# Attention with soft expert routing on one core: slot inputs from 128-token products, x turned in 32-row groups on VectorE

## The chip, the core and the metric

The kernel runs on one core of a Trainium2 chip. Its engines work side by side, each through its own queue in order: TensorE (PE; its weight loads are listed apart as PEld), VectorE (DVE), ScalarE (ACT), GpSimd (POOL) and SyncE (SP), which issues the DMAs. Engines wait for each other by semaphores. The metric is the device time of one execution in microseconds.

## The reference

Eight batches of attention with sigmoid weights give x, one row per token. A soft mixture of experts follows: every one of 32 slots is a softmax-weighted mean over all tokens, eight experts with four slots each transform the slots, and every token is a softmax-weighted mean of the slot outputs.

```python
scores = q @ k.T / sqrt(64) - log(448)              # B=8, H=12, S=448, head 64
attn = 1 / (1 + exp(-scores));  x = attn @ v        # x: 3584 tokens x 768
logits = x @ phi                                    # 3584 x 32 slots
d = exp(logits - logits.max(0)); d /= d.sum(0) + 1e-9
slot_input = d.T @ x                                # 32 x 768, over all tokens
h = relu(slot_input[e] @ w1[e]); slot_out[e] = h @ w2[e]   # 8 experts, 4 slots each
c = exp(logits - logits.max(1)); c /= c.sum(1) + 1e-9
out = c @ slot_out                                  # 3584 x 768, all float32
```

## The kernel before

**Attention.** Heads go in pairs: `p` counts 48 pairs, six to a batch, and x of a pair is a tile of 128 rows (two heads of 64) by 448 tokens, so channels lie on the partitions. Keys go in chunks of 128; the 64 keys left over of two neighbouring pairs share a unit (`c == NFK`, tiles `vl`). `seq` lists the units, seven per two pairs and 21 per batch. The loop of line 365 makes one pass per unit: `score(u)` (four products in 64x64 tiles of TensorE into a PSUM tile `sc`, then one sigmoid on ACT), and, two units later (`LAG`), `weigh(u)` (four products into `av0` for an even pair or `av1` for an odd one). `sc` has two buffers, `av0` and `av1` one each. After a pair's last full chunk `evac_a` copies the first half of its sum to `xr`; when the other half is there, `evac_b` adds it. For an even pair the second comes one pass later, behind the left-over keys; for an odd pair at once.

**Slots.** After a batch, `logits_job` multiplies phi with x into four groups of 32 rows: row 32j + s holds slot s over a share of the tokens given by `COLS`. Each of the 128 rows keeps its own running maximum in `mz` (`softmax_a`), and `softmax_b` forms exp on ACT from two sigmoids, `softmax_c` ends it on DVE. `turn` transposes x of a pair in place by 32x32 blocks on DVE, six instructions of 128x448 per batch. `spread` writes the weights to DRAM and reads them back four times, once for each group of 32 partitions, since `slot_mm` multiplies in 32x32 tiles: 56 products of 32x192 per batch, into two PSUM tiles. `slot_job` adds them to `acc` after scaling. For the last batch `last_job` does all this without the bounce, brings the four maxima of a slot together, and forms `sT`, the slot inputs.

**Order.** PE, DVE, ACT and SP run in the order of the program text. The tables `early`, `middle` and `late` (lines 352 to 363) say in which pass, counted from a batch's end, each job is written.

**Experts and output.** 56 of 128 weight tiles are loaded during attention; eleven more take the place of attention's buffers, and the others follow as tiles come free. `w1_part` (line 430), `w2_step` and `out_tile` run over them.

Of the kernel before, what the change touches and what calls it, by code (L numbers as in the profile page):

```python
# [18 lines left out]
P = 128  # L19
NFK = 3  # L20
LAG = 2
W_STEPS = 140
# [15 lines left out]
SL0 = 256  # L38
COLS = (0, 128, 256, 352, 448)
# [7 lines left out]
def soft_moe_attention(ctx: ExitStack, tc: tile.TileContext, qk, v, vl, phi, w1, w2, cst, out):  # L47
# [12 lines left out]
    mz = cpool.tile([P, 2], F32, name="mz")  # L60
    rz = cpool.tile([P, 1], F32, name="rz")
    lt_all = cpool.tile([P, B, P], F32, name="lt_all")
    sT = cpool.tile([P, NKC, NSLOT], F32, name="sT")
    acc = small.tile([P, DM], F32, name="acc")
    phi_t = small.tile([P, 256], F32, name="phit")
    phi_sb = phi_t[:, 0:NKC * NSLOT].rearrange("p (k s) -> p k s", k=NKC)
    nc.vector.memset(acc[:, 0:S], 0.0)
# [28 lines left out]
    with ExitStack() as actx:  # L96
# [4 lines left out]
        bounce = actx.enter_context(tc.tile_pool(name="bounce", bufs=2, space=bass.MemoryType.DRAM))  # L101
# [3 lines left out]
        xr = xp.tile([P, 3, 3, S], F32, name="xr")  # L105
        lgs = xp.tile([P, P], F32, name="lgs")
        nc.vector.memset(lgs[64:128, 96:128], NEG)
        qkts, vts, vls, avs, atts, dts, drs = {}, {}, {}, {}, {}, {}, {}

        def x_of(p):  # L110
            b, hp = divmod(p, NPR)
            return xr[:, (2 * b + hp // 3) % 3, hp % 3, :]
# [56 lines left out]
        def evac_a(p):  # L169
            nc.vector.tensor_copy(x_of(p), avs[p][:, 1, 0:S])  # L170
# [5 lines left out]
        def evac_last(p):  # L176
            x, av = x_of(p), avs.pop(p)
            for t in (slice(0, COLS[2]), slice(COLS[2], S)):
                nc.scalar.copy(x[:, t], av[:, 1, t])
# [5 lines left out]
        def turn(p):  # L185
            nc.vector.transpose(x_of(p), x_of(p))  # L186

        def logits(lg, b, pairs, js=(3, 2, 1, 0)):
            for hp in pairs:
                for j in js:  # L190
                    nc.tensor.matmul(  # L191
                        lg[32 * j:32 * j + 32, 0:COLS[j + 1] - COLS[j]], phi_sb[:, hp, :],
                        x_of(b * NPR + hp)[:, COLS[j]:COLS[j + 1]],
                        start=(hp == 0), stop=(hp == NPR - 1))

        def logits_job(b):
            lg = ps_sc.tile([P, 2, 512], F32, name="sc")[:, 0, :]
            logits(lg, b, range(NPR))
            nc.vector.tensor_copy(lgs[0:64, :], lg[0:64, 0:P])
            nc.vector.tensor_copy(lgs[64:128, 0:96], lg[64:128, 0:96])  # L200
            softmax_a(b)

        def softmax_a(b):
            t1 = small.tile([P, 2, 132], F32, name="t1")
            zt, ls = t1[:, 0, :], lgs[:]
            if b == 0:
                nc.vector.tensor_reduce(out=mz[:, 0:1], in_=ls, axis=AX.X, op=ALU.max)
            else:
                m1 = small.tile([P, 2], F32, name="m1")
                nc.vector.tensor_reduce(out=m1[:, 0:1], in_=ls, axis=AX.X, op=ALU.max)  # L210
                nc.vector.tensor_copy(m1[:, 1:2], mz[:, 0:1])
                nc.vector.tensor_tensor(out=mz[:, 0:1], in0=m1[:, 0:1], in1=m1[:, 1:2], op=ALU.max)
                nc.vector.tensor_tensor(out=zt[:, P:P + 1], in0=m1[:, 1:2], in1=mz[:, 0:1], op=ALU.subtract)
            nc.vector.tensor_scalar(zt[:, 0:P], ls, mz[:, 0:1], None, op0=ALU.subtract)
            dts[b] = t1
# [7 lines left out]
        def softmax_c(b):  # L223
# [5 lines left out]
            if b == 0:  # L229
                nc.vector.tensor_reduce(out=mz[:, 1:2], in_=pe[:, 0:P], axis=AX.X, op=ALU.add)  # L230
            else:
# [3 lines left out]
                    out=mz[:, 1:2], in0=mz[:, 1:2], scalar=pe[:, P:P + 1], in1=zb[:], op0=ALU.mult, op1=ALU.add)  # L235
            nc.vector.transpose(lt_all[:, b, :], lgs[:])

        def spread(b):
            flat = bounce.tile([P, P], F32, name="zd")
            nc.sync.dma_start(flat[:], dts[b][:, 0, 0:P])  # L240
            drs[b] = xp.tile([P, 4, NBK * BLK], F32, name="dr")
            for a in range(4):
                nc.sync.dma_start(drs[b][32 * a:32 * a + 32, :, :], flat[:].rearrange("(j i) n -> i j n", j=4))

        def slot_mm(b, sl=None):
            if sl is None:
                sl = [ps_av.tile([P, 2, 512], F32, name="av1"), ps_sc.tile([P, 2, 512], F32, name="sc")]
            t = 2 * b % 3
            y = xr[:, t:t + 2] if t < 2 else xr[:, 2::-2]
            for c in range(NBK):  # L250
                for a in range(4):
                    for j in range(4 if c < 3 else 2):
                        k = COLS[j] // BLK + c
                        nc.tensor.matmul(  # L254
                            sl[a // 2][32 * j:32 * j + 32, a % 2, SL0:SL0 + NPR * BLK],
                            drs[b][32 * a:32 * a + 32, j, c * BLK:(c + 1) * BLK],
                            y[32 * a:32 * a + 32, :, :, k * BLK:(k + 1) * BLK],
                            start=(c == 0), stop=(c == (3 if j < 2 else 2)))
            return sl

        def acc_of(g):
            return acc[:, g * HALF:(g + 1) * HALF].rearrange("p (a n) -> p a n", a=2)

        def slot_job(b):
            sl = slot_mm(b)
            for g in range(2):
                part = sl[g][:, :, SL0:SL0 + NPR * BLK]
                if b == 0:
                    nc.vector.tensor_copy(acc_of(g), part)
                else:  # L270
                    nc.vector.scalar_tensor_tensor(
                        out=acc_of(g), in0=acc_of(g), scalar=dts[b][:, 1, P:P + 1], in1=part,
                        op0=ALU.mult, op1=ALU.add)

        def last_job(b, lgt, pw):
            lg = lgt[:, 0, 0:P]
            pa = lgt[:, 1, :]
            ps = pw[:, 0, 0:NKC * NSLOT]
            t1 = small.tile([P, 2, 132], F32, name="t1")
            pe, zt = t1[:, 0, 0:P], t1[:, 1, 0:P]  # L280
            m1 = small.tile([P, 2], F32, name="m1")
            cw = small.tile([P, 8 + 2 * NSLOT], F32, name="cw")
            sw = cw[:, 8:].rearrange("p (z s) -> p z s", z=2)
            nc.vector.tensor_reduce(out=m1[:, 0:1], in_=lg, axis=AX.X, op=ALU.max)
            nc.vector.tensor_scalar(cw[:, 0:1], m1[:, 0:1], mz[:, 0:1], -1.0, op0=ALU.max, op1=ALU.mult)
            nc.scalar.activation(pe, lg, AF.Exp, bias=cw[:, 0:1])
            nc.scalar.activation(cw[:, 1:2], mz[:, 0:1], AF.Exp, bias=cw[:, 0:1])
            nc.tensor.matmul(pa[0:1, 0:P], cw[:, 0:1], ident, start=True, stop=True)
            warm(pw, 1)
            turn(b * NPR + 5)  # L290
            nc.vector.transpose(zt, pe)
            tr = [ps_av.tile([P, 2, 512], F32, name="av1"), ps_sc.tile([P, 2, 512], F32, name="sc")]
            for j in range(4):
                r = slice(32 * j, 32 * j + 32)
                nc.tensor.matmul(tr[j // 2][:, j % 2, 0:P], csb[r, 128:256], zt[r, :], start=True, stop=True)
            mrow = small.tile([1, 1, NSLOT], F32, name="mrow")
            nc.vector.tensor_reduce(
                out=mrow[:], in_=pa[0:1, 0:P].rearrange("o (j s) -> o s j", j=4), axis=AX.X, op=ALU.min)
            drs[b] = xp.tile([P, 4, NBK * BLK], F32, name="dr")
            nc.scalar.copy(drs[b][:, 0:2, :], tr[0][:, :, 0:P])  # L300
            nc.vector.tensor_copy(drs[b][:, 2:4, :], tr[1][:, :, 0:P])
            for j in range(4):
                nc.tensor.matmul(pa[32 * j:32 * j + 32, P:P + 1], mrow[:, 0, :], csb[0:1, 0:1], start=True, stop=True)
            slot_mm(b, tr)
            nc.vector.tensor_tensor(out=cw[:, 2:3], in0=pa[:, P:P + 1], in1=cw[:, 0:1], op=ALU.subtract)
            nc.scalar.activation(cw[:, 3:4], cw[:, 2:3], AF.Exp)
            nc.vector.tensor_scalar(sw[:, 0], sel4, cw[:, 3:4], None, op0=ALU.mult)
            nc.vector.tensor_scalar(sw[:, 1], sw[:, 0], cw[:, 1:2], None, op0=ALU.mult)
            total = xr[:, 1, 0:2, :].rearrange("p a n -> p (a n)")[:, 0:DM]
            for g, copy in enumerate((nc.scalar.copy, nc.vector.tensor_copy)):  # L310
                copy(total[:, g * HALF:(g + 1) * HALF].rearrange("p (a n) -> p a n", a=2),
                     tr[g][:, :, SL0:SL0 + NPR * BLK])
            for a in range(4):
                nc.tensor.matmul(
                    ps[32 * a:32 * a + 32, :], sw[:, 1], acc[:, a * 192:a * 192 + 192], start=True, stop=False)
            for a in range(4):
                nc.tensor.matmul(  # L317
                    ps[32 * a:32 * a + 32, :], sw[:, 0], total[:, a * 192:a * 192 + 192], start=False, stop=True)
            nc.vector.transpose(sT[:].rearrange("p k s -> p (k s)"), ps)
# [3 lines left out]
                out=cw[:, 5:6], in0=mz[:, 1:2], scalar=cw[:, 1:2], in1=cw[:, 4:5], op0=ALU.mult, op1=ALU.add)  # L323
# [290 lines left out]
```

## Time and profile before

| | |
|---|---|
| median of 3 runs | 397.16 us (396.82 to 438.41) |
| the profiled execution | 398.36 us, span of its instructions 396.6 us, mean granted clock 0.968 |
| busy over the span | PE 371.8 us, ACT 204.1, DVE 159.1, POOL 2.3 |
| DMA queue 1 | 96.92 MB, 71.1% of the 16 engines' span |
| slot products (L254) | 896 records, 36.1 us of busy time |
| transposes of x (L186) | 48, 27.8 us on DVE |
| copies of x (L170) and adds (L174) on DVE | 47 each, 29.4 and 28.9 us |
| bounce of slot weights | 7 writes and 28 reads of 64 KB |

Each group of a profile has its line, engine, operation, output and inputs, count, busy time and mean length. Records of PE are pipelined, two to a product here, so their busy times overlap; when a stage of PE begins and ends is read from the chain or the timeline. The median and the profiled execution differ by 1.2 us, and the slowest of the three runs is far from the others.

### The profile page before, as it was taken

The page shows a single profiled execution, that of the slowest core. Times are in us where ns is not written, and L with a number is a line of the kernel's source. Part 1 is how long each engine was busy: PE and PEld are TensorE (multiplying, and loading weights), DVE is VectorE, ACT ScalarE, POOL GpSimd, SP SyncE. Part 2 cuts the span into 40 slices and gives each one's busy share as a digit, 9 for nine tenths or more (in the row PEclk, how much of TensorE's full clock was granted, in tenths as well). Part 3 has the DMA queues.
Part 4 walks back from the last instruction along what each step waited for, and adds up shares of the span by engine and source line. Part 5 has one row for each costly group of instructions (what it writes and reads, how often), then busy time and mean ns, then how long its engine had stood idle before and what let it go on. Part 6 is the DMA issues. An engine that isn't in the chain of part 4 may idle for free.

```text
span 396.6 us, 11091 instructions
## 1 busy us (share of the span) xinstructions
PE 371.8 (94%) x4748; PEld 163.8 (41%) x4748; DVE 159.1 (40%) x375; ACT 204.1 (51%) x261; POOL 2.3 (1%) x12
## 2 busy tenths in 40 slices
PE   8999999999999999999999999999989979999760
PEld 5333444434343434434343444344345633422330
DVE  0212642273246326423722553274254771232460
ACT  4666656565656566565656565655641113422450
POOL 0000000000000000000000000000001000000000
PEclk9999999999999999999999999999999996999885
DMA  7677468757565876675586557443275999999998
GB/s 248 204 251 250 149 197 257 247 168 257 204 217 170 273 236 206 190 258 184 181 284 216 199 160 249 136 130 117 69 260 198 404 399 401 400 402 399 389 396 293
DMA packets 47425, 97.62 MB, mean 246 GB/s; under 512 B 5008, under 2 KB 23568, under 8 KB 47376
## 3 DMA queue, kind: packets, MB, share of 16 engines
q1 hardware_dynamic: 47376, 96.92, 71.1%
q8 instruction: 37, 0.61, 0.6%
q14 instruction: 12, 0.10, 0.1%
HBM read 85.43 MB, written 11.47 MB: 244 GB/s over the span
## 4 chain that ended last, share of the span: by engine, by line
PE 80%; DMA 14%; ACT 1%; DVE 1%; issue 1%; SPq 0%; ACTq 0%
PE sc L138 31%; PE av L167 31%; DMA wa<-in_w_dram 10%; PE ph L434 5%; PE sc L191 3%; PE av L254 3%; PE sc L254 2%; DMA wb<-in_w_dram 2%; PE ph L499 1%; DMA zd<-t 1%; PE pt L499 1%; PE av L344 1%; PE av L154 1%; DMA dr<-zd 1%; PE av L183 0%
## 5 line engine op out<-in xcount | busy, mean ns | idle before, releaser
L142 ACT ACTIVATE att<-sc,nbias 128x896 f32<-128x896 f32 x168 | 169.0, 1006 | 114.9 <-PE sc L138 114.9
L138 PE MATMUL sc<-qkt 64*64 64x448 f32 x1344 | 157.4, 539 | 0.4 <-ACT att L142 0.4
L167 PE MATMUL av<-att,v 64*64 64x448 f32 x1128 | 131.4, 536 | 0.0
L170 DVE COPY xr<-av 128x448 f32<-128x448 f32 x47 | 29.4, 625 | 135.2 <-PE av L167 135.2
L138 PEld LDWEIGHTS sc<-qkt 64*64 64x64 f32 x1344 | 49.9, 133 | 72.8 <-issue 66.5
L167 PEld LDWEIGHTS av<-att,v 64*64 64x64 f32 x1128 | 43.1, 133 | 62.9 <-issue 62.9
L174 DVE TENSOR_TENSOR xr<-xr,av 128x448 f32<-128x448 f32 x47 | 28.9, 615 | 15.7 <-PE av L167 14.9
L186 DVE STREAM_TRANSPOSE xr<-xr 128x448 f32<-128x448 f32 x48 | 27.8, 619 | 1.3 <-PE sc L191 1.3
L167 PE MATMUL av<-att,vl 64*64 64x448 f32 x192 | 23.2, 554 | 0.0
L434 PE MATMUL ph<-wa,sT 128*32 128x256 f32 x336 | 18.9, 379 | 0.8 <-DVE lt_all L320 0.8
L500 ACT COPY wa<-ph 128x384 f32<-128x384 f32 x27 | 12.8, 479 | 11.5 <-PE ph L499 9.3
L254 PE MATMUL av<-xr,dr 32*32 32x192 f32 x448 | 18.4, 355 | 0.3 <-ACT dr L300 0.3
L500 DVE COPY wa<-pt 128x384 f32<-128x384 f32 x27 | 14.2, 556 | 9.1 <-PE pt L499 8.7
L254 PE MATMUL sc<-xr,dr 32*32 32x192 f32 x448 | 17.7, 354 | 0.2 <-DMA dr<-zd 0.2
L434 PEld LDWEIGHTS ph<-wa,sT 128*32 128x32 f32 x336 | 10.9, 110 | 8.2 <-PE av L317 1.1
L254 PEld LDWEIGHTS av<-xr,dr 32*32 32x32 f32 x448 | 11.0, 107 | 6.6 <-issue 4.9
L499 PE MATMUL ph<-st,wb 128*128 128x384 f32 x28 | 12.7, 454 | 1.0 <-DVE st L529 1.0
L167 PEld LDWEIGHTS av<-att,vl 64*64 64x64 f32 x192 | 6.3, 131 | 15.6 <-DVE xr L170 13.1
L191 PE MATMUL sc<-xr,phit 128*32 128x96 f32 (+1 forms) x384 | 12.3, 262 | 0.0
L191 PEld LDWEIGHTS sc<-xr,phit 128*32 128x32 f32 x384 | 9.9, 110 | 5.8 <-issue 5.6
L499 PE MATMUL pt<-st,wb 128*128 128x384 f32 x28 | 10.6, 377 | 1.6 <-DVE st L529 1.6
L536 PE MATMUL po<-wa,acc 128*32 128x384 f32 x84 | 9.9, 579 | 0.0
(122 smaller groups left out, 178.6 us busy)
## 6 DMA issues: line engine op xcount, KB each, us to landing
wa<-in_w_dram SPq DMA_DIRECT2D x112, 384.0 KB, 6.7
qkt<-in_qk_dram SPq DMA_DIRECT2D x48, 448.0 KB, 3.6
out_dram<-wa SPq DMA_DIRECT2D x27, 384.0 KB, 5.6
v<-in_v_dram SPq DMA_DIRECT2D x48, 192.0 KB, 3.1
wb<-in_w_dram SPq DMA_DIRECT2D x16, 384.0 KB, 5.3
dr<-zd SPq DMA_DIRECT2D x28, 64.0 KB, 1.9
vl<-in_vl_dram SPq DMA_DIRECT2D x24, 64.0 KB, 3.2
zd<-t SPq DMA_DIRECT2D x7, 64.0 KB, 3.6
```

Source lines behind the costliest of these rows:

```text
L138: nc.tensor.matmul(sc[64 * t:64 * t + 64, h, 0:S], qkts[pt][r, S + k0:S + k0 + 64], qkts[pt][r, 0:S], start=True, stop=True)
L142: nc.scalar.activation(att[:], sc[:, :, 0:S], AF.Sigmoid, bias=nbias[:], scale=QSCALE)
L167: nc.tensor.matmul(o[r, t, 0:S], w, att[row, h, :], start=start, stop=stop)
L170: nc.vector.tensor_copy(x_of(p), avs[p][:, 1, 0:S])
L174: nc.vector.tensor_tensor(out=x_of(p), in0=x_of(p), in1=av[:, 0, 0:S], op=ALU.add)
L186: nc.vector.transpose(x_of(p), x_of(p))
L191: nc.tensor.matmul(lg[32 * j:32 * j + 32, 0:COLS[j + 1] - COLS[j]], phi_sb[:, hp, :], x_of(b * NPR + hp)[:, COLS[j]:COLS[j + 1]], start=(h ...
L254: nc.tensor.matmul(sl[a // 2][32 * j:32 * j + 32, a % 2, SL0:SL0 + NPR * BLK], drs[b][32 * a:32 * a + 32, j, c * BLK:(c + 1) * BLK], y[32 ...
L434: nc.tensor.matmul(ph[32 * j:32 * j + 32, 0:256], sT[:, kc, :], utile[("w1", e, j, kc // 3)][:, kc % 3 * 256:(kc % 3 + 1) * 256], start=(k ...
L499: nc.tensor.matmul(pf[:, 0:HALF], ct_of(m), st[:], start=True, stop=True)
L500: (nc.scalar.copy, nc.vector.tensor_copy)[n % 2](ov, pf[:, 0:HALF])
L536: nc.tensor.matmul(po[32 * fl:32 * fl + 32, 0:HALF], hT[e][:, 4 * g + fl, :], ut, start=(n == 0), stop=(n == 2 * E - 1))
```

## The change

The slot products now take 128 tokens at a time. Logits are cut so that row 32j + s holds slot s over every fourth block of 32 tokens; a 32x32 transposition of the weights then gives tiles with 128 tokens on the partitions, and `slot_mm` makes 16 products in 128x32 tiles, 192 columns each, into one bank. The bounce (`spread`) is gone. For this x must have tokens on the partitions too: `turns` and `turns3` transpose, on DVE, blocks from row group a of `xs` to row group g of a new tile `ys`, 16 instructions of 32 partitions for one pair or for three pairs at once, 64 per batch in place of six. They stand in a list `todo`, and `work` writes some of them at the end of each pass by a budget (`PACE`). All four groups of a slot share one maximum, found by `softmax_a` for each batch. `evac_a`, the first copy of x, goes from DVE to ACT. `softmax_b` and `softmax_c` move one pass down, `logits_job` and `slot_job` stay. In the last batch PE transposes the last pair, and the scaling needs no second set of products. On the host, the order of queries and of the rows of w1 changes.

```diff
+PACE = 32
+SLOT_AT = 9
+TR = 3
...
         def evac_a(p):
-            nc.vector.tensor_copy(x_of(p), avs[p][:, 1, 0:S])
+            nc.scalar.copy(x_of(p), avs[p][:, 1, 0:S])
...
-        def turn(p):
-            nc.vector.transpose(x_of(p), x_of(p))
+        def turns(p):
+            t, k = divmod(p % NPR, TR)
+            for a in range(4):
+                r = slice(32 * a, 32 * a + 32)
+                for g in range(4):
+                    todo.append((nblk(g), lambda r=r, a=a, g=g: nc.vector.transpose(
+                        blocks(ys[t][32 * g:32 * g + 32, k, 0, :], a, nblk(g)), blocks(xs[t][r, k, :], g, nblk(g)))))
+        def turns3(t):
...
+                    todo.append((TR * nblk(g), lambda r=r, a=a, g=g: nc.vector.transpose(
+                        blocks3(ys[t][32 * g:32 * g + 32, :, 0, :], a, nblk(g)), blocks3(xs[t][r, :, :], g, nblk(g)))))
...
         def softmax_a(b):
...
+            m1 = small.tile([NSLOT, 8], F32, name="m1")
+            for j in range(4):
+                r = slice(32 * j, 32 * j + 32)
+                nc.vector.tensor_reduce(out=m1[:, j:j + 1], in_=ls[r, 0:BLK * nblk(j)], axis=AX.X, op=ALU.max)
+            if b:
+                nc.vector.tensor_copy(m1[:, 4:5], mz[0:32, (b - 1) % 2:(b - 1) % 2 + 1])
+            nc.vector.tensor_reduce(out=m1[:, 5:6], in_=m1[:, 0:5 if b else 4], axis=AX.X, op=ALU.max)
+            for j in range(4):
+                nc.vector.tensor_copy(new[32 * j:32 * j + 32, :], m1[:, 5:6])
...
+        def slot_mm(sl, zt):
             for c in range(NBK):
+                for j in range(4):
+                    h = slice(64 * (j % 2), 64 * (j % 2) + 64)
+                    nc.tensor.matmul(
+                        sl[32 * j:32 * j + 32, 0:SLN], zt[:, c * BLK:(c + 1) * BLK], ys[j // 2][:, :, c, h],
+                        start=(c == 0), stop=(c == NBK - 1))
...
         def last_job(b, lgt, pw):
...
+            for c in range(NBK):
+                n = P if c < NBK - 1 else 64
+                nc.tensor.transpose(out=px[0:n, c * P:(c + 1) * P], in_=x_of(p)[:, c * P:c * P + n], identity=ident)
+            nc.tensor.matmul(pa[0:1, 0:P], m1[:, 0:1], ident, start=True, stop=True)
...
+            slot_mm(sl, zt)
+            nc.vector.scalar_tensor_tensor(
+                out=acc[:], in0=acc[:], scalar=cw[:, 1:2], in1=sl[:, 0:SLN], op0=ALU.mult, op1=ALU.add)
...
+        for b in range(B):
+            u = b * per_b + LAG
+            late[u + 10] = [lambda: turns3(0)]
+            for k, o in ((3, 14), (4, 18), (5, 21)):
+                if b < B - 1 or k < 5:
+                    late[u + o] = [lambda p=b * NPR + k: turns(p)]
         for b in range(B - 1):
+            u = (b + 1) * per_b + LAG
+            early[u + 1] = [lambda b=b: logits_job(b)]
+            middle[u + 2] = [lambda b=b: softmax_b(b)]
+            late[u + 3] = [lambda b=b: softmax_c(b)]
+            late[u + SLOT_AT] = [lambda b=b: slot_job(b)]
+            rate[u] = rate[u + 1] = rate[u + 3] = 0
+        def work(n):
+            while todo and n > 0:
+                k, turn = todo.popleft()
+                turn()
+                n -= k + 2
...
                     if p == NP - 1:
-                        for k in range(5, 0, -1):
-                            turn(p - k)
+                        work(B * S)
...
             for f in late.get(i, ()):
                 f()
+            work(rate.get(i, PACE))
```

Three places show how the order moves. The first is DVE in the second batch, from the end of the slot products to the logits: `acc` is the slot sum, `xr` (later `x_93`, `x_94`) is x, `av_...` the PSUM sums of the pairs, `lgs` the logits. Before:

```order
L269 COPY acc<-av_625 128x384
L269 COPY acc<-sc 128x384
L174 TENSOR_TENSOR xr<-xr,av_591 128x448
L170 COPY xr<-av_692 128x448
L174 TENSOR_TENSOR xr<-xr,av_692 128x448
L170 COPY xr<-av_750 128x448
L174 TENSOR_TENSOR xr<-xr,av_750 128x448
L170 COPY xr<-av_791 128x448
L174 TENSOR_TENSOR xr<-xr,av_791 128x448
L199 COPY lgs<-sc 64x128
L200 COPY lgs<-sc 64x96
```

In the changed kernel, from the add of the batch's fourth pair to that of the fifth (`y_95` and `y_96` are the two halves of the transposed x; `x2` means two alike in a row):

```order
L185 TENSOR_TENSOR x_94<-x_94,av_711 128x448
L208 STREAM_TRANSPOSE y_95<-x_93 32x12x32
L208 STREAM_TRANSPOSE y_95<-x_93 32x3x3x32 x2
L208 STREAM_TRANSPOSE y_95<-x_93 32x12x32 x2
L208 STREAM_TRANSPOSE y_95<-x_93 32x3x3x32 x2
L201 STREAM_TRANSPOSE y_96<-x_94 32x4x32 x2
L201 STREAM_TRANSPOSE y_96<-x_94 32x3x32 x2
L201 STREAM_TRANSPOSE y_96<-x_94 32x4x32 x2
L201 STREAM_TRANSPOSE y_96<-x_94 32x3x32 x2
L201 STREAM_TRANSPOSE y_96<-x_94 32x4x32 x2
L185 TENSOR_TENSOR x_94<-x_94,av_781 128x448
```

Between the slot products and the logits DVE had only copies and adds; now seven long and ten short transposes stand between the adds of p3 and p4, nine long ones ahead of that, and 18 short ones between the adds of p4 and p5.

The second place is ACT around the end of the first batch, where `att` are the sigmoids of the passes and `t_...` those of the slot softmax. Before:

```order
L142 ACTIVATE att<-sc,nbias 128x896 x25
L220 ACTIVATE t_474<-t_474 128x128
L221 ACTIVATE t_474<-t_474 128x128
L142 ACTIVATE att<-sc,nbias 128x896 x21
L220 ACTIVATE t_881<-t_881 128x129
```

In the changed kernel:

```order
L181 COPY x_94<-av_413 128x448
L153 ACTIVATE att<-sc,nbias 128x896 x3
L247 ACTIVATE t_523<-t_523 128x128
L248 ACTIVATE t_523<-t_523 128x128
L181 COPY x_93<-av_491 128x448
L153 ACTIVATE att<-sc,nbias 128x896 x4
L181 COPY x_93<-av_579 128x448
```

The copies of x now stand behind the sigmoid of the same pass, and the first copy of a batch behind the two sigmoids of the softmax as well.

The third place is PE at the first left-over unit of the second batch (`vl` are the left-over values). Before, with what each waits for:

```order
L138 MATMUL sc<-qkt 64x448 [waits Activation_49]
L138 MATMUL sc<-qkt 64x448 x3
L167 MATMUL av_442<-att,vl 64x448 [waits DMAHW4_49,DVE_49]
L167 MATMUL av_442<-att,vl 64x448
L167 MATMUL av_521<-att,vl 64x448 x2
```

In the changed kernel:

```order
L149 MATMUL sc<-qkt 64x448 [waits Activation_49]
L149 MATMUL sc<-qkt 64x448 x3
L178 MATMUL av_491<-att,vl 64x448 [waits DMAHW4_49,Activation_49]
L178 MATMUL av_491<-att,vl 64x448
L178 MATMUL av_579<-att,vl 64x448 x2
```

The first left-over product waited for the copy on DVE; now it waits for the copy on ACT.

202 lines of the change are left out of this document (74 added, 128 removed).

## Prediction

> **What bounds the kernel now.** I read the page's engine table first, then the windows by stage, then the chain of waits, and last the timeline at the places that the change touches.
>
> ```profile
> span 396.6 us, 11091 instructions
> 77.00:113.00 36.00, 36.00 (x500) 15.36 (x496) 15.31 (x34) 21.63 (x24) 0.00 (x0) 1.00 0.68 224
> 301.00:321.00 20.00, 19.61 (x350) 11.75 (x354) 14.81 (x57) 3.17 (x12) 0.79 (x4) 1.00 0.97 363
> 321.00:396.00 75.00, 54.94 (x388) 22.76 (x380) 25.33 (x63) 23.86 (x56) 0.00 (x0) 0.86 1.01 387
> ```
>
> The columns after the length are PE, PEld, DVE, ACT, POOL, then granted clock, DMA share and GB/s. In the second row, one batch of attention, PE is busy for all 36 us at a granted clock of 1.00, DVE for 15.3 and ACT for 21.6: PE sets the pace, and DVE has 20 us to spare. From 301 us on the DMA share is 0.97 to 1.01: the rest streams weights and output, has a fixed length, and starts when the first expert product starts. So the time is that start plus 95.2 us. What the change does to PE's path ahead of it counts in full, and what it does behind it counts little.
>
> ```profile
> 13.93 0.75 PE sc L138 x8
> 16.94 0.75 PE sc L138 x8
> ...
> 41.44 1.45 PE sc L191 x42
> 42.89 0.91 PE sc L138 x8
> 56.06 0.75 PE av L167 x8
> 58.94 0.91 PE sc L138 x8
> 77.36 1.45 PE sc L191 x42
> ```
>
> The chain (start, length, what) gives the unit of account. One pass of the loop, four score and four weighing products, takes (16.94 − 13.93)/2 = 1.505 us; logits take 1.45; a batch takes 77.36 − 41.44 = 35.92. The slot products fill 56.81 to 58.94, which is 2.13. I number the passes of a batch by the unit that is weighed, 0 to 20, and its pairs p0 to p5; the logits of a batch stand ahead of pass 1 of the next batch, its slot products behind pass 9.
>
> **Slot products: a gain.** 56 products in 32x32 tiles become 16 in 128x32 tiles. Each column tile streams 4 × 192 = 768 columns in turn. The logits stream 6 × 128 = 768 per column tile in the same 128x32 tiles and took 1.45 us. So I take 1.45, bounds 1.3 and 2.13 (no gain): −0.68 us, 7 times, −4.8 us. The DRAM bounce that goes costs PE nothing now, since PE was never idle.
>
> **First copy of x on ScalarE: a new wait.** PE's product of the left-over keys (c = 3, passes 3, 10 and 17) waits for `evac_a` of the same pair.
>
> ```profile
> 10.52 0.93 PE L138 MATMUL sc<-qkt 64*64 64x448 f32 x8
> 11.58 1.01 ACT L142 ACTIVATE att<-sc,nbias 128x896 f32<-128x896 f32 x1 [0.47 <-PE sc L138]
> 12.27 0.62 DVE L170 COPY xr<-av 128x448 f32<-128x448 f32 x1 [10.77 <-PE av L167]
> 12.95 0.21 PEld L167 LDWEIGHTS av<-att,vl 64*64 64x64 f32 x8 [0.77 <-DVE xr L170]
> L489 ACT CAST wb<-pt 128x448 fp32r<-128x448 f32 x4 | 2.1, 532 | 4.6 <-PE pt L480 4.6
> 45.19 0.31 ACT L221 ACTIVATE t<-t 128x128 f32<-128x128 f32 x1
> ```
>
> Call T the end of the score issue, 10.52 + 0.75 = 11.27. Today the copy runs on an idle DVE at T + 1.00 and releases PE at T + 1.68, already 0.18 late. On ACT it is queued behind the sigmoid, which runs from T + 0.31 to T + 1.32; the same shape took 0.53 there (L489), so PE is released at about T + 1.92: +0.25 us. That holds at pass 17 in every batch (7 × 0.25 = 1.75, the last one counted with the end) and at passes 3 and 10 of the first batch (0.5). Later, pass 10 is covered by the slot products. At pass 3 two more sigmoids of the softmax (L220 and L221, 0.65 together) now stand between, since `softmax_b` has moved one pass down: T + 2.57, +0.9 us, 7 times, 6.3 us. On ACT what is queued behind the copy is the next sigmoid, but ACT waits 0.47 us for PE in each pass today (L142's row), which covers it.
>
> **Transposes on DVE: the largest term.** Six transposes of 128 partitions per batch become 64 of 32 partitions: 16 over three pairs (384 or 288 elements) and 48 over one (128 or 96).
>
> ```profile
> L228 DVE STREAM_TRANSPOSE t<-t 128x128 f32<-128x128 f32 x7 | 2.2, 311 | 0.2
> L186 DVE STREAM_TRANSPOSE xr<-xr 128x448 f32<-128x448 f32 x48 | 27.8, 619 | 1.3 <-PE sc L191 1.3
> L174 DVE TENSOR_TENSOR xr<-xr,av 128x448 f32<-128x448 f32 x47 | 28.9, 615 | 15.7 <-PE av L167 14.9
> 49.09 2.21 DVE L186 STREAM_TRANSPOSE xr<-xr 128x448 f32<-128x448 f32 x4
> 42.94 0.28 DVE L199 COPY lgs<-sc 64x128 f32<-64x128 f32 x1 [1.65 <-PE sc L191]
> 43.23 0.26 DVE L200 COPY lgs<-sc 64x96 f32<-64x96 f32 x1
> ```
>
> A line through L228 (128 elements, 0.311) and L186 (448, 0.619) gives 0.557, 0.465, 0.311 and 0.280 us for 384, 288, 128 and 96 elements. Whether an instruction costs all of that depends on overlap. Four L186 in a row fill 2.21 us, not 4 × 0.62, so each starts some 0.087 before the last one ends: they all start at partition 0. L199 and L200 need nothing of each other, but L200 starts at partition 64, and it starts 0.29 after L199, which took 0.28: no overlap, 0.014 more. In the changed kernel each transpose writes another group of 32 partitions than the one ahead of it (g runs innermost), so I price them as L200: full length plus 0.014.
>
> [...]
>
> The order puts 16 long and 28 short transposes, and the adds (L174) of p3 and p4, between p2's add at pass 10 and p5's. DVE is then a queue that never empties: 0.25 (start after the weighing) + 0.615 (p2) + 8 × 0.557 + 8 × 0.465 + 14 × 0.311 + 14 × 0.280 + 44 × 0.014 + 2 × 0.615 + 0.615 = 19.8 us after pass 10. PE comes to the last pair of the logits after 10 passes (15.05), pass 17's 0.48, one more pass (1.505) and five sixths of 1.45: 18.2 us. So the logits wait 1.6 us for p5's add, 7 times: 11.2 us. In the before kernel DVE was idle there. Behind it four more transposes (1.2 us) delay the logits' copies and so the softmax; its sigmoids, and with them the copy at pass 3, come some 0.3 us later: 7 × 0.3 = 2.1.
>
> **The end.**
>
> ```profile
> 286.38 0.98 PE L167 MATMUL av<-att,vl 64*64 64x448 f32 x8
> 288.95 1.30 PE L191 MATMUL sc<-xr,phit 128*32 128x96 f32 x40
> 293.19 0.29 DVE L284 TENSOR_REDUCE m<-sc 128x1 f32<-128x128 f32 x1 [1.02 <-PE sc L191]
> 295.92 0.68 PE L254 MATMUL av<-xr,dr 32*32 32x192 f32 x8 [0.29 <-ACT dr L300]
> 298.89 0.55 PE L254 MATMUL sc<-xr,dr 32*32 32x192 f32 x4
> 300.67 0.38 DVE L319 STREAM_TRANSPOSE sT<-av 128x192 f32<-128x192 f32 x1 [0.62 <-PE av L317]
> 301.39 1.88 PE L434 MATMUL ph<-wa,sT 128*32 128x256 f32 x24 [0.78 <-DVE lt_all L320]
> ```
>
> Today the maximum (L284) starts at 293.19, the slot products at 295.92, the experts at 301.39. With a DVE that keeps up, the maximum stays there, but four PE transposes of p5 stand ahead of its turn into a row, and row, column, exp and transpose follow: slot products at about 296.9, 1 us later than now. Their 1.45 to 2.4 us (they took 3.45 here against 2.13 in a batch), then one add and transpose in place of two copies, eight products and a transpose (1.25 us) put the experts at 299.6 to 300.6: −1.3 us. With the queue above, 16 transposes of the fifth pair (5.0 us) stand ahead of the maximum: p46's add ends 15.5 us after pass 10, which is 276.4 by the old clock, so DVE is free at 296.9, and the maximum starts 3.7 us later than now. PE's transposes are done by then, so the chain behind the maximum is 2.3 us to the slot products, about 2.1 for them and 1.25 to the experts, 5.7 instead of today's 8.2: experts at 302.6, +1.2 us.
>
> **Sum.** −4.8 + 1.75 + 0.5 + 6.3 + 2.1 + 11.2 + 1.2 = +18.3 us on the profiled execution's 398.36, so 416.6; the median of the runs shown is 1.2 lower, so 415.4.
>
> **Rivals.**
>
> (1) The transposes overlap as L186 does. Then each is 0.087 shorter and the 0.014 goes: 44 × 0.101 = 4.4 us less queue, p5's add comes at 15.4 us, ahead of PE, and the terms 11.2, 2.1 and 1.2 give way to 0, 0 and −1.3: −4.8 + 1.75 + 0.5 + 6.3 − 1.3 = +2.5, a median of 399.6, no change. For it: four rows of L186 and DVE's 20 idle us per batch. Against it: L200. The point from which it decides is a mean of 0.352 us per transpose instead of 0.388. Chance 0.22. [...]
>
> (2) Moving between groups of partitions is dearer than any row shows: 0.03 us more per transpose is 1.3 us more wait per batch, some +10 us: 426. Nothing in the profile is for it but that no row does the same. Chance 0.08.
>
> (3) The slot products stay at 2.13 us, since something other than columns per tile sets their length. That is +4.8, inside the forecast's own range. Against it: L191's 1.45 for as many columns.
>
> (4) Both waits fall away, the copy on ACT and the queue on DVE: −4.8 − 1.3, a median of 391. It needs `evac_a` to start ahead of the sigmoid, against its order. Chance 0.08 with all else that is lower.
>
> **How the numbers follow.** The forecast case has 0.62. Its own range is 405 to 424: 0.02 us more or less per transpose is 0.9 us per batch, 6 in all, and with it goes the follow-up at pass 3; the slot bound adds 4.8. Rival 1 reaches from 396 to 404. A range of 397 to 425 holds almost all of the forecast case and most of rival 1, about 0.8. A measurement of this kernel tells about 2%, 7.9 us, from no change. Slower by more: rival 2 and nine tenths of the forecast case, 0.64. Within: rival 1, the forecast's low end and most of rival 4, 0.31. Faster: 0.05.
>
> **What would show it.** Groups of short transposes on DVE whose starts lie their full mean apart (0.32) and not 0.23; DVE above 80% busy in the batch windows; the last logits group of PE waiting for the add on DVE some 1.6 us; the load of the left-over keys waiting for ACT and not DVE; a batch period near 38.3 us, where rival 1 has 36.4; slot products of 1.45 us. The forecast is wrong if DVE sits idle ahead of p5's add, or if PE's first product at pass 3 starts before the copy on ACT ends.

## The result, and the profile after

The changed kernel takes 415.03 us (median of 4 runs, 414.34 to 416.25) against 396.99 us for the kernel before: a ratio of 1.0461, 95% interval 1.0427 to 1.0495. The change makes it slower by 18.0 us; the prediction was 415.4 us. (Runs far from the others of their kernel are left out of the ratios: 438.41 and 409.61 us for the kernel before, 2021 us for the first of the faster versions below.)

The profiled execution took 415.46 us. These are the page's span, the window of one batch, and that of the last stage:

```profile
span 413.7 us, 10213 instructions
81.60:120.00 38.40, 35.51 (x416) 14.63 (x416) 31.13 (x93) 24.22 (x29) 0.00 (x0) 1.00 0.59 191
320.00:413.00 93.00, 73.11 (x713) 33.55 (x710) 39.38 (x114) 26.71 (x68) 0.00 (x0) 0.91 1.00 381
```

In a batch DVE went from 15.3 us busy to 31.1, which is 81%, and PE, which was never idle, now idles 38.40 − 35.51 = 2.89 us. The granted clock is 1.00 there, so nothing of this is the clock's. The last window, the experts, is still held by the DMAs, at a share of 1.00.

The chain of waits gives the period of a batch and the length of the slot products (start, length, what):

```profile
4.59 0.96 PE sc L149 x8
...
58.98 1.44 PE sc L269 x32
...
97.21 1.44 PE sc L269 x32
```

A batch takes 97.21 − 58.98 = 38.23 us, where it took 35.92. The slot products take 1.44 us instead of 2.13. PE's idle time is named by the list of waits (us in total, times, longest):

```profile
PE sc L214 <- DVE x L185: 11.2, 7, 1.6
PE av L178 <- ACT x L181: 6.8, 7, 1.0
PE sc L214 <- DVE sc L390: 3.0, 1, 3.0
```

Seven times the logits (L214) wait 1.6 us for the add of the last pair on DVE; seven times the product of the left-over keys at pass 3 waits 1.0 us for the copy on ACT (L181). The third row is the last batch, and comes below. The timeline shows the first wait in its place:

```profile
76.01 5.07 DVE L201 STREAM_TRANSPOSE y<-x 32x96 f32<-32x96 f32 x17
81.11 0.62 DVE L185 TENSOR_TENSOR x<-x,av 128x448 f32<-128x448 f32 x1
81.78 0.42 PE L214 MATMUL sc<-x,phit 128*32 128x96 f32 x8 [1.60 <-DVE x L185]
```

and the second one:

```profile
86.08 0.31 ACT L247 ACTIVATE t<-t 128x129 f32<-128x129 f32 x1 [0.26 <-DVE t L241]
86.42 0.31 ACT L248 ACTIVATE t<-t 128x129 f32<-128x129 f32 x1
86.64 0.51 ACT L181 COPY x<-av 128x448 f32<-128x448 f32 x1
87.20 0.98 PE L178 MATMUL av<-att,vl 64*64 64x448 f32 x8 [1.01 <-ACT x L181]
```

In the first, short transposes stand back to back ahead of the add that PE waits for; the row has the last 17 of the 18 between the adds of p4 and p5. In the second, the two sigmoids of the softmax stand ahead of the copy on ACT.

### The profile page after: what moved, and what is told of

It is laid out like the page before. It is cut to its first block, busy times and chain, and to the rows that moved or that the text cites. A ratio compares the mean times of both kernels' runs of the same rounds, so it can differ in the third digit from the quotient of the medians.

```text
span 413.7 us, 10213 instructions
## 1 busy us (share of the span) xinstructions
PE 367.8 (89%) x4096; PEld 157.3 (38%) x4096; DVE 279.8 (68%) x816; ACT 223.9 (54%) x306; POOL 3.1 (1%) x14
## 4 chain that ended last, share of the span: by engine, by line
DVE 48%; PE 36%; DMA 5%; issue 4%; ACT 4%; DVEq 0%; ACTq 0%; SPq 0%
DVE y L201 16%; DVE y L208 16%; PE av L178 12%; PE sc L149 11%; DVE x L185 5%; PE po L540 4%; PE sc L269 3%; DMA wa<-in_w_dram 2%; DMA out_dram<-wb 2%; DVE m L232 2%; DMA out_dram<-wa 2%; PE pt L484 1%; DVE mz L238 1%; ACT x L181 1%; DVE tmp L453 1%
## 5 line engine op out<-in xcount | busy, mean ns | idle before, releaser
L201 DVE STREAM_TRANSPOSE y<-x 32x128 f32<-32x128 f32 (+1 forms) x368 | 105.3, 286 | 5.2
L208 DVE STREAM_TRANSPOSE y<-x 32x288 f32<-32x288 f32 (+1 forms) x128 | 66.5, 520 | 2.0
L185 DVE TENSOR_TENSOR x<-x,av 128x448 f32<-128x448 f32 x47 | 29.2, 621 | 35.1 <-PE av L178 29.6
L540 PE MATMUL po<-wa,h 128*32 128x384 f32 x224 | 27.0, 514 | 0.0
L214 PE MATMUL sc<-x,phit 128*32 128x96 f32 (+1 forms) x384 | 14.1, 265 | 14.2 <-DVE x L185 11.2
L181 ACT COPY x<-av 128x448 f32<-128x448 f32 x47 | 24.6, 523 | 0.0
L438 PE MATMUL ph<-wa,phit 128*32 128x256 f32 x336 | 18.5, 379 | 1.3 <-DVE lt_all L320 1.3
L214 PEld LDWEIGHTS sc<-x,phit 128*32 128x32 f32 x384 | 9.6, 110 | 22.0 <-DVE x L185 13.1
L438 PEld LDWEIGHTS ph<-wa,phit 128*32 128x32 f32 x336 | 10.8, 110 | 8.5 <-issue 1.7
L269 PE MATMUL sc<-y,t 128*32 128x192 f32 x256 | 12.1, 329 | 0.0
```

The source lines that it names most:

```text
L181: nc.scalar.copy(x_of(p), avs[p][:, 1, 0:S])
L185: nc.vector.tensor_tensor(out=x_of(p), in0=x_of(p), in1=av[:, 0, 0:S], op=ALU.add)
L201: todo.append((nblk(g), lambda r=r, a=a, g=g: nc.vector.transpose(blocks(ys[t][32 * g:32 * g + 32, k, 0, :], a, nblk(g)), blocks(xs[t][r, ...
L208: todo.append((TR * nblk(g), lambda r=r, a=a, g=g: nc.vector.transpose(blocks3(ys[t][32 * g:32 * g + 32, :, 0, :], a, nblk(g)), blocks3(xs ...
L214: nc.tensor.matmul(lg[32 * j:32 * j + 32, 0:BLK * nblk(j)], phi_sb[:, hp, :], blocks(x_of(b * NPR + hp), j, nblk(j)), start=(hp == 0), sto ...
L269: nc.tensor.matmul(sl[32 * j:32 * j + 32, 0:SLN], zt[:, c * BLK:(c + 1) * BLK], ys[j // 2][:, :, c, h], start=(c == 0), stop=(c == NBK - 1))
```

## The experiments

The theory: per batch the slot products give 0.69 us; the DVE queue, whose transposes do not overlap since each starts in another group of 32 partitions, costs 1.6 us at the logits; the copy on ACT, behind the softmax's sigmoids, costs about 1 us at pass 3. The rival: these waits are only where a slower batch shows (something else, such as the slot products, the copy's engine as such or the load on memory, takes the time), so that taking one away moves the idle time to another place. Each edit is against the changed kernel unless it says otherwise.

**What a transpose of 32 partitions costs.** Thirty-two extra transposes of 32x128, results unused, stand ahead of attention in four groups of eight: the same row group for input and output, then the output's group moves, then the input's, then both.

```diff
+        for n in range(8):
+            nc.vector.transpose(lt_all[0:32, n, :], acc[0:32, 0:P])
+        for n in range(8):
+            g = 32 * (n % 4)
+            nc.vector.transpose(lt_all[g:g + 32, n, :], acc[0:32, 0:P])
+        for n in range(8):
+            g = 32 * (n % 4)
+            nc.vector.transpose(lt_all[0:32, n, :], acc[g:g + 32, 0:P])
+        for n in range(8):
+            g = 32 * (n % 4)
+            nc.vector.transpose(lt_all[g:g + 32, n, :], acc[g:g + 32, 0:P])
```

> The changed kernel with 32 more transposes of 32x128 on DVE ahead of attention, where DVE has nothing else to do, in four groups of eight: input and output both from partition 0; input from 0 and output going round partitions 0, 32, 64, 96; input going round and output at 0; both going round. The theory of the prediction (a change of the group of 32 partitions on either side keeps an instruction from starting before the last one has ended) expects starts about 0.225 us apart in the first group and 0.31 in the three others. A rival, that only a change on both sides or only one of the input does it, expects 0.225 in the second group too. The total time is not the point; it should stay within 1% of the changed kernel's.

The timeline of DVE shows the four groups in that order:

```profile
1.12 1.65 DVE L110 STREAM_TRANSPOSE lt_all<-acc 32x128 f32<-32x128 f32 x8
2.70 2.52 DVE L113 STREAM_TRANSPOSE lt_all<-acc 32x128 f32<-32x128 f32 x8
5.25 2.55 DVE L116 STREAM_TRANSPOSE lt_all<-acc 32x128 f32<-32x128 f32 x8
7.82 2.52 DVE L119 STREAM_TRANSPOSE lt_all<-acc 32x128 f32<-32x128 f32 x8
```

The view of the first line has the lengths (least, median and most, in ns):

```profile
L110 DVE STREAM_TRANSPOSE lt_all<-acc x8: 256/256/299, 1.1 to 2.5; 32x128 f32<-32x128 f32 x8
```

With the group unchanged, eight fill 1.65 us and one takes 0.256, so they start (1.65 − 0.256)/7 = 0.199 apart and overlap by 0.06; some 0.225 was expected. With the output's group alone moving, the input's alone, or both, eight fill 2.52 to 2.55: (2.52 − 0.301)/7 = 0.317 apart (0.301 being the length of this form in the changed kernel, below), the full length and 0.016 more. So in this trace a transpose whose group moves on either side starts only when the one ahead of it has ended, for an output alone too, where the prediction's row of L200 has both sides moving.

**No block transposes at all.** `work` takes the entries off the list and issues nothing; `ys` is zeroed once, so the slot inputs are zero, while all else runs.

```diff
-            nc.gpsimd.memset(y[64:128, :, NBK - 1, :], 0.0)
+            nc.gpsimd.memset(y[:], 0.0)
...
                 k, turn = todo.popleft()
-                turn()
```

> The changed kernel with all block transposes of x on DVE left out (the transposed x is zero then, except for the last pair, so the slot inputs are not the reference's); everything else stands. If the queue of transposes is what holds up the logits, the 11.2 us of logits waits, 1 to 2 us at pass 3 and some 4.5 us in the last batch go: about 398 us, period 36.3 us. A rival by which the new copies on ScalarE or the new slot products cost most of the loss expects it above 407.

It took 395.45 us, ratio to the kernel before 0.9936 (0.9914 to 0.9959). A batch takes 94.05 − 58.06 = 35.99 us:

```profile
58.06 1.44 PE sc L269 x32
...
94.05 1.44 PE sc L269 x32
```

and the only wait of any size that is left for PE is the copy's:

```profile
PE av L178 <- ACT x L181: 4.5, 7, 0.6
```

So the transposes are worth 19.6 us of the 415.0, and the logits' wait is theirs. Yet a batch without them is no shorter than the 35.92 us of the kernel before: what the slot products give goes to the copy's waits, and the 0.6% comes from outside the batches. The wait at pass 3 is 0.6 here and 1.0 with the transposes; by the difference, 0.4 us of it is the softmax being late behind the queue (the prediction had 0.3).

**The softmax behind the copy.** One line: `softmax_b` is written behind the pass's copy, not ahead of it.

```diff
-            middle[u + 2] = [lambda b=b: softmax_b(b)]
+            late[u + 2] = [lambda b=b: softmax_b(b)]
```

> The changed kernel with one thing moved: the two sigmoids of the slot softmax stand behind the copy of x of the same pass on ScalarE, not ahead of it. If PE waits at pass 3 for a copy that is queued behind them, each batch is about 0.95 us shorter, 7 times: 408.3 us, and the wait of PE for the copy there falls from 1.0 us to about 0.2. A rival, that DVE's total work sets the period, expects the gain to come back as a longer wait for the logits: no change.

410.13 us, ratio to the kernel before 1.0313 (1.0275 to 1.0351). The period is 96.73 − 59.41 = 37.32 us, 0.91 less:

```profile
59.41 1.44 PE sc L269 x32
...
96.73 1.44 PE sc L269 x32
```

PE's wait for the copy at pass 3 is gone from the list of waits; the logits' stays:

```profile
PE sc L214 <- DVE x L185: 11.6, 7, 2.0
```

Six of the seven waits are 1.6 us long as before, one is 2.0. The edit gave 4.9 us, where seven times 0.91 would be 6.4: one batch of the profiled execution, from 246.02 on, took 39.34 us, 2.0 more than its neighbours, which is the size of what is missing. It is the batch of the longer wait, and PE's granted clock (the third figure from the end of a window's row) falls to 0.50 behind it, from about 269.7 to 273.0:

```profile
269.21 0.43 PE L214 MATMUL sc<-x,phit 128*32 128x96 f32 x8 [1.99 <-DVE x L185]
271.00:272.00 1.00, 1.00 (x12) 0.46 (x8) 0.94 (x4) 0.57 (x1) 0.00 (x0) 0.50 0.00 0
```

Whether the runs without a trace had such a batch too stays open.

**A slower pace.** With a budget of 28 instead of 32 per pass, 37 instead of 44 transposes stand ahead of p5's add; the rest comes behind the logits.

```diff
-PACE = 32
+PACE = 28
```

> The changed kernel with the budget of transposes per pass at 28 instead of 32: the same instructions, but 37 instead of 44 ahead of the add of the batch's last pair. If that queue is the cause, it is 2.1 us shorter there, the logits no longer wait, one more transpose stands ahead of the copies of the logits, and a batch takes 1.2 us less: about 406.5 us. The rival, DVE's total work sets the period, expects no change.

404.21 us, ratio 1.0165 (1.0132 to 1.0197). The same work, differently spread, is 10.8 us faster. The period is 95.04 − 58.28 = 36.76 us, 1.47 less, and the seven waits of the logits for the add are gone, while those for the copy are as before:

```profile
58.28 1.44 PE sc L269 x32
...
95.04 1.44 PE sc L269 x32
...
PE av L178 <- ACT x L181: 6.8, 7, 1.0
```

So it isn't that DVE has too much to do in a batch (81% busy), but where the add stands in its queue.

**Both together.**

```diff
-PACE = 32
+PACE = 28
...
-            middle[u + 2] = [lambda b=b: softmax_b(b)]
+            late[u + 2] = [lambda b=b: softmax_b(b)]
```

> The changed kernel with both moves: budget 28 and the softmax sigmoids behind the copy. If the two waits are separate places on PE's path, their gains add: 36.77 us per batch (budget 28) less 0.9, 35.9, and about 398 us. If one only hides the other, the time stays near the better of the two, 404 us.

398.3 us, ratio 1.0016 (0.9994 to 1.0038): level with the kernel before. The period is 93.30 − 57.43 = 35.87 us, which is 2.36 less than the changed kernel's 38.23; the two single edits gave 1.47 and 0.91, together 2.38. They add up, so the two waits are two causes, and neither turned into another wait. The rival falls for the two of them.

**The copy back on DVE.** `evac_a` alone as it was before.

```diff
-            nc.scalar.copy(x_of(p), avs[p][:, 1, 0:S])
+            nc.vector.tensor_copy(x_of(p), avs[p][:, 1, 0:S])
```

> The changed kernel with the first copy of x back on VectorE. The queue theory expects it slower still: three more copies of 0.62 us stand ahead of the last pair's add, and the copies that PE waits for stand in the queue of transposes: some 39.5 us per batch, 424 us. A rival, that the copy on ScalarE is what costs the time, expects it at 406 us or less.

428.44 us in one run, 13.4 more than the changed kernel and 4 more than expected. A batch takes 100.06 − 60.52 = 39.54 us by the chain, as expected; the 4 us more lie in the last batch, where the slot products come 31.4 us behind those of the batch before, 4.1 later than in the changed kernel. The copy now stands in DVE's queue among the transposes:

```profile
PE av L178 <- DVE x L181: 25.6, 12, 6.3
PE sc L214 <- DVE x L185: 2.9, 3, 1.0
```

The logits' wait shrinks because PE already lost more, up to 6.3 us at a time, at the product behind the copy. The longest of these waits is in the last batch, and behind it PE is slower: the left-over products take 1.77 us there and the score that follows 1.49, where the chain has 0.98 and 0.75 for the same two behind the wait before it. With these transposes on DVE the copy belongs on ACT.

**The copy on ACT alone.** The kernel before, with only `evac_a` moved:

```diff
-            nc.vector.tensor_copy(x_of(p), avs[p][:, 1, 0:S])
+            nc.scalar.copy(x_of(p), avs[p][:, 1, 0:S])
```

> The kernel before with one edit: the copy of the numerator into the rows of x runs on ScalarE instead of VectorE; block transposes, slot products, DRAM bounce and rates stay as they were before. By the prediction's terms for the copy, it ends later where its product is awaited or where ScalarE has a softmax in hand: 0.25 us at pass 17 of each of the 8 batches and at pass 10 of the first (0.5 there), so about 8 x 0.25 + 0.5 = 2.5 us on the path, some 399.5 us where the kernel before has 397, ratio near 1.006. If the wait of 1.0 us at pass 3, seen in the changed kernel, belongs to the copy's engine alone, 7 x 1.0 us more: about 406 us, ratio near 1.02. If the copy costs nothing by itself and the losses come only with the longer VectorE queue, the ratio is 1.000.

399.24 us, ratio to the kernel before 1.0035 (1.0010 to 1.0060): 1.4 us, interval 0.4 to 2.4. The expected 2.5 us lies 0.1 above the interval and "no cost" 0.4 below it, so it is some cost, and less than was expected; 9 us is far outside. The same batch of this kernel, and of the kernel before:

```profile
200.00:236.00 36.00, 35.83 (x500) 15.34 (x496) 11.60 (x28) 23.98 (x30) 0.00 (x0) 1.00 0.68 224
```

```profile
200.00:236.00 36.00, 36.00 (x504) 15.36 (x496) 15.23 (x33) 21.63 (x24) 0.00 (x0) 1.00 0.66 216
```

PE idles 0.17 us per batch. By the starts in the timeline 0.11 of it is at pass 17, where the prediction's sum has 0.25, and 0.06 at pass 3. The copy's engine costs little by itself; the 1.0 us at pass 3 needs the softmax ahead of it.

**Three versions that aim to be faster.** The first lays all six pairs of a batch into two groups of three (`turns3` for both: 32 long transposes per batch in place of 64), with a pace of 26, the softmax behind the copy, the slot products one pass later, and in the last batch two pairs turned together with five transposes behind the maximum.

```diff
-PACE = 32
-SLOT_AT = 9
+PACE = 26
+SLOT_AT = 10
...
-            for k, o in ((3, 14), (4, 18), (5, 21)):
-                if b < B - 1 or k < 5:
-                    late[u + o] = [lambda p=b * NPR + k: turns(p)]
+            if b < B - 1:
+                late[u + 21] = [lambda: turns3(1)]
+            else:
+                late[u + 17] = [lambda: turns3(1, 2)]
...
-            middle[u + 2] = [lambda b=b: softmax_b(b)]
+            late[u + 2] = [lambda b=b: softmax_b(b)]
...
-        for i in range(u + 10, u + 31):
-            rate[i] = PACE + 8
+        rate[u + 17] = 12
...
```

> The changed kernel with the transposes of the second half of a batch done over three pairs too (32 long instructions per batch instead of 16 long and 48 short), written behind the last pair's add, slot products one pass later, the softmax sigmoids behind the copy, and in the last batch two pairs at once with five transposes behind the maximum. The queue theory expects no logits wait, a period of about 35.6 us against 35.92 of the kernel before, and a shorter end: 393 us, 1% below the kernel before. If fewer and longer transposes do not keep the queue short, it stays above 397.

395.87 us, ratio 0.9955 (0.9935 to 0.9975), faster than the kernel before by less than 2%. Its batches take 130.26 − 94.27 = 35.99 us, no less than those of the run with both edits (35.87). Its slot products stand at another place and are 0.2 us longer, so what halving the number of transposes gives by itself isn't separated here. Its chain and one row of its waits:

```profile
94.27 1.64 PE sc L270 x32
130.26 1.64 PE sc L270 x32
...
PEld av L178 <- ACT x L181: 21.5, 24, 1.2
```

The slot products take 1.64 there, and the weight loads wait for the copy 24 times instead of 17: with the slot products one pass later they no longer cover the copy at pass 10. To see if that wait sets the period, the left-over products of the pair that needs no copy were issued first:

```diff
-            for t in range(2):
+            for t in ((0, 1) if c < NFK else (1, 0)):
```

> As the run before it, and PE's left-over products of the pair that need no copy are issued first. If PE waits at passes 3 and 17 for the copy alone, up to 0.2 us at each is covered: 0.3 us per batch, 391 us. If the order of four products that run side by side does not matter, the same as the run before it.

396.27 us, ratio 0.9975 (0.9955 to 0.9994), with a period of 35.98: nothing gained, against 391 expected. The loads' wait for the copy did shrink, from 21.5 us to 4.8:

```profile
PEld av L178 <- ACT x L181: 4.8, 9, 0.8
```

So it didn't set the period. Why the slot products take 0.2 us longer at this place stays open.

The third keeps the short transposes, the pace of 28 and the slot products' place (the run with both edits above), and changes only the last batch, like the first version: pairs p3 and p4 turned together from pass 17 on, a budget of 12 at that pass and PACE behind it, where the changed kernel has PACE + 8 from pass 10 of this batch on, and five transposes behind the maximum.

```diff
-            for k, o in ((3, 14), (4, 18), (5, 21)):
-                if b < B - 1 or k < 5:
+            if b < B - 1:
+                for k, o in ((3, 14), (4, 18), (5, 21)):
                     late[u + o] = [lambda p=b * NPR + k: turns(p)]
+            else:
+                late[u + 17] = [lambda: turns3(1, 2)]
...
-        for i in range(u + 10, u + 31):
-            rate[i] = PACE + 8
+        rate[u + 17] = 12
...
-                        work(B * S)
+                        while len(todo) > 5:
+                            work(1)
...
```

> The run with the pace of 28 and the softmax behind the copy (398.3 us, ratio 1.002, 35.87 us a batch), with the last batch rearranged: the logits tile is cleared earlier, the last two pairs are turned together, two rows deep, from pass 17 on, and five block transposes stand behind the maximum. By the theory that the end of the changed kernel lost 3.0 us at the logits behind the clearing and 1.4 us in the weighing that ran slow after that idle time, the batches keep 35.9 us and the end gives up to 4 us: about 394 us, ratio near 0.991. If the end is bound elsewhere (the chain behind the maximum), it stays at 398, ratio 1.00.

395.12 us, ratio to the kernel before 0.9942 (0.9920 to 0.9964), the fastest here, though not clear of the first version's 0.9955. The logits' tile is cleared at the same place of the program as before, but fewer transposes stand ahead of that: it comes 1.8 us behind the start of the last score, where it came 4.7 behind it. The 3 us wait is gone, and so is the slow weighing behind it:

```profile
57.16 1.44 PE sc L270 x32
...
93.03 1.44 PE sc L270 x32
...
288.16 1.30 PE L215 MATMUL sc<-x,phit 128*32 128x96 f32 x40
289.39 1.72 PE L165 MATMUL av<-att,v 128*64 128x448 f32 x8
```

The experts start at 299.06 us, 3.8 earlier than with both edits alone (302.86). This and its 35.87 us a batch leave it 0.6% ahead of the kernel before, 4.8% ahead of the change as it was made (395.12 to 415.03). Which of the moves in the last batch brings how much of the 3.8 us isn't separated.

## Why the prediction was right, point by point

**Slot products.** Forecast 1.45 us from the logits' columns, measured 1.44, in every batch. Rival 3 (they stay at 2.13) is out. The gain of 0.69 us per batch was there and was outweighed.

**Transposes on DVE.** The two groupings of the lines on DVE, with every shape apart (count, busy us and mean ns, idle before):

```profile
L201 DVE STREAM_TRANSPOSE y<-x 32x128 f32<-32x128 f32 x184 | 55.4, 301 | 2.6
L201 DVE STREAM_TRANSPOSE y<-x 32x96 f32<-32x96 f32 x184 | 49.9, 271 | 2.6
L208 DVE STREAM_TRANSPOSE y<-x 32x384 f32<-32x384 f32 x64 | 36.4, 568 | 1.2
L208 DVE STREAM_TRANSPOSE y<-x 32x288 f32<-32x288 f32 x64 | 30.2, 471 | 0.8
```

Forecast 0.311, 0.280, 0.557 and 0.465; measured 0.301, 0.271, 0.568 and 0.471. The short ones are shorter and the long ones longer, and for the 44 ahead of the add the mean, with 0.014 between two, is (8 × 0.568 + 8 × 0.471 + 14 × 0.301 + 14 × 0.271)/44 + 0.014 = 0.385 against 0.388. The starts lie 5.07/17 = 0.298 apart in a run that mixes both short forms: full length and a little, no overlap. Rival 1 needed a mean below 0.352 and is out, and so are rival 2, which needed some 0.42, and rival 4, which needed both waits gone. The logits' wait came out at 1.6 us, as forecast. What this reading took from one pair of rows (L199 and L200) was then measured apart, and holds (0.317 us from start to start where the group moves, 0.199 where it stays).

**Copy on ACT.** At pass 3 the forecast was 0.9 and 0.3 for the softmax that comes late, 1.2 in all; PE's row has 1.0 us. Leaving the transposes out gave 0.6 and 0.4 for the two parts. At pass 17, 0.25 was forecast; there the product starts 1.04 us behind the score ahead of it (109.15 to 110.19), where the kernel before has 0.93, so 0.11. Together the batch has 35.92 − 0.68 + 0.25 + 1.2 + 1.6 = 38.29 by the terms, and 38.23 by the chain. The parts are less exact than the sum: the logits, from their start to the next score, went from 1.44 to 3.26 us, 1.82 more for the 1.6 of the wait; pass 3 is 1.05 longer and pass 17 0.11. In the sum these misses cancel.

**The end: the term that was mis-sized, +1.2 forecast, +2.2 measured.** From the last score to the first expert product the changed kernel takes 318.53 − 302.15 = 16.38 us, the kernel before 301.39 − 287.18 = 14.21. The rows of the changed kernel:

```profile
302.15 0.93 PE L149 MATMUL sc<-qkt 64*64 64x448 f32 x8
306.26 0.62 DVE L185 TENSOR_TENSOR x<-x,av 128x448 f32<-128x448 f32 x1
306.89 0.09 DVE L390 MEMSET sc<- 64x32 f32 x1
306.91 4.78 DVE L201 STREAM_TRANSPOSE y<-x 32x128 f32<-32x128 f32 x16
307.03 1.56 PE L214 MATMUL sc<-x,phit 128*32 128x96 f32 x40 [3.04 <-DVE sc L390]
308.52 3.10 PE L165 MATMUL av<-att,v 128*64 128x448 f32 x8
312.91 0.29 DVE L292 TENSOR_REDUCE m<-sc 128x1 f32<-128x128 f32 x1 [1.22 <-PE sc L214]
318.53 1.50 PE L438 MATMUL ph<-wa,phit 128*32 128x256 f32 x24 [1.33 <-DVE lt_all L320]
```

The prediction let DVE's queue alone release the maximum (L292): 16 transposes behind p46's add, DVE free at 296.9 by the old clock. By the new clock that is 296.9 + (302.15 − 287.18) = 311.87, and DVE was free at 306.91 + 4.78 = 311.69, as forecast. But the maximum started at 312.91, released by PE. The step that failed is that PE would be through by then: "PE's transposes are done by then", says the prediction, but PE ended the logits only at 312.83, and its transposes (L297) start at 313.08. The logits' tile is cleared by L390, which stands on DVE behind the same add, so that all logits waited 3.04 us, not the last pair's alone. Then the weighing of four products took 3.10 us where it took 1.72 before. The granted clock, microsecond by microsecond, goes with it (the rows from 309 and 310 us, not shown, have 0.50 too):

```profile
307.00:308.00 1.00, 0.97 (x38) 0.97 (x40) 0.96 (x4) 0.00 (x0) 0.00 (x0) 0.96 0.69 276
308.00:309.00 1.00, 1.00 (x10) 0.43 (x6) 0.96 (x4) 0.00 (x0) 0.00 (x0) 0.50 0.08 16
...
311.00:312.00 1.00, 1.00 (x8) 0.45 (x5) 0.67 (x3) 0.33 (x2) 0.00 (x0) 0.83 0.00 0
```

After 3.04 us without work, and 0.9 us after it resumed, PE got half its clock for about 3.4 us (0.83 in the last row is a third of it at half). The wait alone would not have failed the step: the kernel before took 293.19 − 288.95 = 4.24 us from the start of the logits to the maximum, and 307.03 + 4.24 = 311.27 is still ahead of DVE. The 1.64 us beyond that are the slower logits (1.56 us, before 1.30) and weighing. Behind the maximum the chain took 318.53 − 312.91 = 5.62 us, forecast 5.7, but by parts that cancel: 2.78 us to the slot products (forecast 2.3, for which it shows no working), 1.5 for them (2.1) and 1.3 to the experts (1.25). The slot products' upper bound of 2.4 fits 1.45 × 3.45/2.13, and the 3.45 us of the kernel before ran at half clock, 0.50 from 296 to 299 us, which the prediction did not see:

```profile
297.00:298.00 1.00, 1.00 (x52) 0.88 (x58) 0.00 (x0) 0.00 (x0) 0.00 (x0) 0.50 0.72 277
```

The version with the rearranged last batch has neither the 3.04 us wait nor the half clock behind it (granted clock 1.00 from 284 to 296 us), and starts the experts 3.8 us earlier than the same kernel without it.

**The sum.** The experts start 318.53 − 301.39 = 17.14 us later, and what follows takes 413.7 − 318.53 = 95.2 us in both kernels. The end's error of +1.0 is set off by others on the way there: up to the last score the change costs 14.97 us, where the terms have 18.3 − 1.2 = 17.1. Four places make up these 2.1 us. PE reaches the third score 0.83 us earlier (6.63 in place of 7.46): its first products start 0.26 earlier, since the sum `acc` that DVE clears ahead of them is 192 columns wide now and not 448 (0.22 us in place of 0.43), and the rest was not traced. The copy on ACT costs 0.11 and not 0.25 us at the three left-over units of the first batch, 0.42 together. The terms of a batch were 0.06 too high six times, 0.36. And the kernel before has one batch of 257.46 − 221.05 = 36.41 us, 0.49 longer than its others, which the changed kernel doesn't have. That the forecast met the time to 0.4 us is partly luck, since these cancel; the mechanism and its two large terms don't rest on it.

## What to carry to other kernels

An engine with idle time left (DVE here, 81% busy in a batch) can still take the time: what counts is what stands ahead of the one instruction that another engine awaits, and here the same transposes cost 10.8 us more or less by whether 44 or 37 of them stood ahead of an add. Price many small instructions by whether they overlap (here 0.199 or 0.317 us from one to the next), read from rows whose partitions move as theirs will. When a step is moved to another queue, look at each place where its result is awaited and at what else was moved to stand ahead of it there.

## What the hardware showed that was not expected

DVE transposes of 32x128 that stay in one row group start 0.199 us apart, and 0.317 as soon as the group of the input or of the output alone changes: 60% more for the same work. A wait of 3.04 us on PE was followed by some 3.4 us at half clock, in which the four products of a weighing took 3.10 us instead of 1.72. The length of the gap alone doesn't tell when: one of 1.99 us in the run with the softmax behind the copy was followed by half clock too, and the kernel before went to 0.50 from 296 to 299 us with no gap above 1.12 us ahead of it, while none of the changed kernel's seven waits of 1.60 us was. What decides it stays open.
